# A fused windowed-attention and squared-ReLU FFN kernel: opening laid out by hand with w_out loaded ahead of chunk 2, and q and k of chunks 4 to 11 turned by the DMA crossbar

## Chip, cores, metric

One core of a Trainium2 chip (trn2). The metric is device time of one execution in microseconds (us), median of several. "Span" is first to last instruction in the profile; in the profiled runs it is 1.7 to 1.9 us shorter than the time of the same execution (before: span 239.2, time 241.05).

## The reference

```python
# q, k, v: (batch 4, heads 8, seq 768, dim 64), float32;  n_global 8, n_local 96
scores = q @ k^T / sqrt(64);  rel = i - j
keep   = (j < 8) | ((rel >= 0) & (rel < 96))
dist   = 96 where global and not local, else |rel|
a      = softmax(where(keep, scores - slope[h] * dist, -1e9))
x      = (a @ v) as (3072 tokens, 512)
out    = square(relu(x @ w_in)) @ w_out        # w_in 512x2048, w_out 2048x512
```

## The kernel before

The 3072 tokens are 12 chunks of 256. A chunk's attention needs q and k with the head dimension on partitions, so each is turned; then come masked scores, exp, values, and a transposed chunk `xt` of x. `f1(c)` is the first FFN product of a chunk (8 pieces, each 8 matmuls of 256 columns, into `hps`), `f2(c)` the second (8 pieces of 4 matmuls of 512 columns, into `yps`). Each engine runs its instructions in the order of the program text, so the text is the schedule. `place(main, side, slots)` puts side job i ahead of main job `slots[i]`; jobs in `later` (mostly VectorE) are emitted ahead of the next job.

```python
    def turn_q(c, h0=0, h1=H, by=None):
        ck = chunks[c]
        ...                                            # cut: new tile ck.q
        trp = bank([P, H, P], "trq", FP16)
        for h in range(h0, h1):
            nc.tensor.transpose(out=trp[:, h, :], in_=ck.sq[:, h, :], identity=ident)
        hh = slice(h0, h1)
        (by or nc.scalar.copy)(out=ck.q[:, 1, hh, :], in_=trp[:, hh, :])
        ...                                            # cut: two VectorE copies, later
    # turn_k: the same for k, then (later) four VectorE copies that build keys kb

    def second(c, j, m0):
        ck = chunks[c]
        if m0 == 0:
            ck.yps = ps_y.tile([P, d_model], FP32, name="yps", tag="y")
        for m in range(m0, m0 + 4):
            nc.tensor.matmul(ck.yps, lhsT=ck.h2[:, m, j * P:(j + 1) * P],
                             rhs=w_out_sb[:, m, :], start=m == 0, stop=m == NFT - 1)
        ...                                            # cut: copy and store y
    def f2(c):
        return [lambda j=j, m0=m0: second(c, j, m0) for j in range(2)
                for m0 in range(0, NFT, 4)]

    ORDER = (0, 2, 3, 1, 6, 4, 5, 7)   # of attention: 0, 1 scores; 2..5 values; 6, 7 xt

        load(0)
        load_w_in(0, 512)
        load(1)
        fill_dist()
        for f in range(512, d_ff, 512):
            load_w_in(f, f + 512)
        load(2)
        for m in range(0, NFT, 4):
            load_w_out(m, m + 4)
        load(3)
        ...                                            # cut: attention of chunk 0
        run(place(f1(0), ...))                         # beside attention of chunk 1
        run(place(f1(1), ...))                         # beside attention of chunk 2
        run(place(f2(0), ...))                         # beside attention of chunk 3
        for c in range(1, NC):
            if c + 5 < NC:
                load(c + 5)
            main = zip_jobs(f2(c), f1(c + 1)) if c + 1 < NC else f2(c)
            ...                      # cut: beside it attention c + 3, turning of c + 4
```

The loads convert float32 to fp16 on the way and are issued by GpSimd (POOL).

The softmax here doesn't subtract the row's maximum and nothing guards it: scores larger than these inputs give would overflow.

## Time and profile before

| | before |
|---|---|
| time, median (range) | 240.07 us (239.79 to 240.2) |
| first FFN matmul | 22.0 us |
| steady stretch | 62 to 228.7 us |
| one loop with turning / without | 17.54 / 16.66 us |

The page of the kernel before: its span, busy time by engine, and two rows of its 40 slices of 6 us (busy tenths).

```profile
span 239.2 us, 5383 instructions
...
PE 221.9 (93%) x2214; PEld 155.1 (65%) x2214; DVE 152.4 (64%) x409; ACT 143.6 (60%) x256; POOL 38.6 (16%) x51
...
PE   4666988979899999999999999999999999999993
...
DMA  6999999994968159158249110110110111101112
```

TensorE (PE) is full from the twelfth slice on and has holes before that, while DMA is full in slices 2 to 9. The engine times by stage of the kernel before say the same in us (columns: stretch, its length, busy time and count of each engine, granted clock, DMA share, GB/s; the DMA share adds up packet times, which overlap, so it can pass 1):

```profile
core 0: us, PE busy (x) PEld busy (x) DVE busy (x) ACT busy (x) POOL busy (x), PEclk, DMA share, GB/s
22.00:62.00 40.00, 35.17 (x427) 26.19 (x426) 30.15 (x83) 31.54 (x61) 13.95 (x16) 1.00 1.43 170
62.00:79.50 17.50, 17.50 (x185) 12.40 (x186) 13.88 (x38) 11.26 (x20) 2.63 (x3) 1.00 0.86 107
149.70:167.30 17.60, 17.60 (x187) 12.51 (x186) 12.40 (x35) 11.42 (x22) 0.00 (x0) 1.00 0.09 32
```

From 62 us on, only less TensorE work makes the kernel faster. "Busy" overlaps pipelined matmuls, so for the stage before it work must be counted in pieces: at the steady pace 22 to 62 us holds 32.5 us of work. What turning costs in a loop is in the chain of waits of the kernel before (start, us, what):

```profile
167.28 0.97 PE yps L341 x4
...
169.12 0.45 PE trq L190 x8
...
177.02 0.45 PE trk L205 x8
...
184.82 0.97 PE yps L341 x4
```

Eight transposes of q take 0.45 us on the path, and eight of k another 0.45. The head of the kernel, from the same chain:

```profile
17.62 1.02 ACT kx L207
...
18.66 0.29 DVE kb L216
...
20.21 0.43 DVE tm L292
...
20.69 0.40 PE trx L304 x2
21.09 0.97 PE sp L261 x16
22.05 3.52 PE hps L329 x16
```

VectorE (DVE) builds chunk 1's keys before it normalises chunk 0's last heads, and the FFN waits for that. The first 16 FFN matmuls then take 3.52 us, where 16 later take 1.75: single ones last up to 421 ns, against a median of 273. (The clock record of this trace begins at 26.1 us, so the 1.00 shown for 22 to 62 us does not cover them.) Three more lines of the kernel before, one from its instructions in order of time and two from what the trace says of the tile of w_in:

```profile
24.80 0.89 POOL L178 DMA_DIRECT2D sq<-in_q_dram  x1 [1.72 <-DMA w_in_sb<-in_moe_w_in_dram]
...
L362 POOL DMA_DIRECT2D w_in_sb<-in_moe_w_in_dram x4: 760/792/815, 4.2 to 9.2; - x4
...
DMA to landing us min/median/max: 7.2/12.2/15.1
```

GpSimd's next load, issued at 24.8 us, had waited for a piece of w_in. The last piece was issued at 9.2 us and took the longest, 15.1 us, so it landed at 24.3 us.

### The profile page before, as it was taken

How to read it: one execution, taken by the hardware profiler on the slowest of the kernel's cores; microseconds unless marked ns; L12 is line 12 of the kernel's file. 1: busy time of each engine (PE TensorE's matmuls, PEld its weight loads, DVE VectorE, ACT ScalarE, POOL GpSimd, SP SyncE). 2: the span in 40 equal slices, each digit the busy share in tenths (PEclk: the TensorE clock that was granted, in tenths of full speed). 3: DMA queues.
4: the chain of work that ended last, by engine and by line, in shares of the span. 5: the costliest groups of instructions: out<-in, count | busy, mean ns of one | idle time of the engine just before them, and what ended most of it. 6: DMA issues, size and time to landing. Idle time of an engine off the chain costs nothing.

```text
span 239.2 us, 5383 instructions
## 1 busy us (share of the span) xinstructions
PE 221.9 (93%) x2214; PEld 155.1 (65%) x2214; DVE 152.4 (64%) x409; ACT 143.6 (60%) x256; POOL 38.6 (16%) x51
## 2 busy tenths in 40 slices
PE   4666988979899999999999999999999999999993
PEld 1554776846567767777676777767766676766651
DVE  7676689766967765567768755658758564333231
ACT  2975996957755764864764774784684564233310
POOL 8842534212302102102102000000000000000000
PEclk9999999999999999999999999999999999999998
DMA  6999999994968159158249110110110111101112
GB/s 61 192 193 203 192 207 187 182 181 83 167 98 84 51 89 91 48 87 88 57 79 90 44 47 0 47 45 3 44 47 0 47 45 47 43 1 47 44 44 88
DMA packets 45144, 20.26 MB, mean 85 GB/s; under 512 B 37952, under 2 KB 42048, under 8 KB 45120
## 3 DMA queue, kind: packets, MB, share of 16 engines
q0 software_dynamic: 41664, 13.63, 51.0%
q1 hardware_dynamic: 3456, 6.29, 6.8%
q8 instruction: 17, 0.28, 0.5%
q14 instruction: 7, 0.06, 0.1%
HBM read 27.26 MB, written 6.29 MB: 140 GB/s over the span
## 4 chain that ended last, share of the span: by engine, by line
PE 82%; ACT 8%; DVE 6%; DMA 2%; issue 1%; POOL 0%; POOLq 0%
PE yps L341 34%; PE hps L329 33%; PE sp L261 5%; PE av L285 4%; ACT ex L268 4%; PE trx L304 2%; DMA sq<-in_q_dram 2%; PE trq L190 2%; PE trk L205 2%; ACT hr L332 2%; DVE tm L292 1%; ACT kx L207 1%; ACT qx L192 1%; DVE qx L195 1%; DVE qx L196 1%
## 5 line engine op out<-in xcount | busy, mean ns | idle before, releaser
L329 PE MATMUL hps<-xt,w_in_sb 128*128 128x256 f16 x768 | 101.1, 276 | 0.0
L341 PE MATMUL yps<-w_out_sb,h 128*128 128x512 f16 x384 | 97.3, 379 | 0.0
L332 ACT ACTIVATE hr<-hps 128x512 f16<-128x512 f32 x96 | 58.9, 617 | 62.3 <-PE hps L329 58.0
L329 PEld LDWEIGHTS <-w_in_sb 128*128 128x128 f16 x768 | 72.7, 99 | 18.5 <-issue 0.2
L333 DVE TENSOR_TENSOR h<-hr 128x512 f16<-128x512 f16 x96 | 40.5, 422 | 43.9 <-ACT hr L332 43.4
L268 ACT ACTIVATE ex<-sp 128x512 f16<-128x512 f32 x96 | 49.4, 609 | 8.3 <-PE sp L261 8.3
L341 PEld LDWEIGHTS <-h 128*128 128x128 f16 x384 | 34.8, 98 | 26.6
L271 DVE TENSOR_TENSOR phat<-ex,mask 128x1024 f16<-128x1024 f16 x48 | 33.0, 691 | 20.7 <-ACT ex L268 20.7
L285 PEld LDWEIGHTS <-phat 128*128 128x128 f16 x384 | 18.8, 101 | 8.6 <-DVE phat L271 2.0
L292 DVE TENSOR_TENSOR tm<-av,rec 128x256 f16<-128x256 f32 x48 | 20.4, 425 | 1.7
L285 PE MATMUL av<-vodd,phat 128*128 128x65 f16 x256 | 18.5, 201 | 2.5 <-DVE vodd L238 1.5
L345 DVE COPY y<-yps 128x512 f32<-128x512 f32 x24 | 16.4, 685 | 5.4 <-PE yps L341 5.4
L306 ACT CAST xt<-trx 128x512 f16<-128x512 f32 x24 | 14.6, 608 | 8.5 <-PE trx L304 8.5
L261 PE MATMUL sp<-qx,kx 64*128 64x128 f16 x256 | 15.5, 232 | 2.9 <-DVE kx L207 1.3
L178 POOL DMA_DIRECT2D sq<-in_q_dram x12 | 10.7, 892 | 44.6 <-PE trq L190 40.3
L261 PEld LDWEIGHTS <-kx 64*128 64x128 f16 x256 | 10.5, 100 | 9.3 <-issue 6.8
L178 POOL DMA_DIRECT2D sk<-in_k_dram x12 | 10.5, 876 | 33.9 <-PE trk L205 29.1
L304 PE MATMUL trx<-perm,tm 128*128 128x128 f16 x96 | 10.6, 226 | 4.7 <-DVE tm L292 4.7
L304 PEld LDWEIGHTS <-tm 128*128 128x128 f16 x96 | 7.3, 99 | 8.8 <-DVE tm L292 6.2
L192 ACT COPY qx<-trq 128x1024 f16<-128x1024 f16 x11 | 11.6, 1054 | 1.6 <-PE trq L190 1.6
L207 ACT COPY kx<-trk 128x1024 f16<-128x1024 f16 x11 | 11.8, 1069 | 0.8 <-PE trk L205 0.8
L285 PE MATMUL av<-veven,phat 128*128 128x65 f16 x128 | 11.3, 194 | 0.0
(55 smaller groups left out, 132.5 us busy)
## 6 DMA issues: line engine op xcount, KB each, us to landing
out_dram<-y SPq DMA_DIRECT2D x24, 256.0 KB, 2.0
sq<-in_q_dram POOLq DMA_DIRECT2D x12, 256.0 KB, 6.3
sk<-in_k_dram POOLq DMA_DIRECT2D x12, 256.0 KB, 6.9
sv<-in_v_dram POOLq DMA_DIRECT2D x12, 256.0 KB, 7.5
w_in_sb<-in_moe_w_in_dram POOLq DMA_DIRECT2D x4, 512.0 KB, 12.2
w_out_sb<-in_moe_w_out_dram POOLq DMA_DIRECT2D x4, 512.0 KB, 17.2
```

The source lines that it names most:

```text
L178: nc.gpsimd.dma_start(out=dst, in_=src[ck.b, :, ck.u * CH:(ck.u + 1) * CH, :].rearrange("h (p e) d -> p h (e d)", e=2))
L261: nc.tensor.matmul(sp[ek][:, e, s, :], lhsT=ck.keys[rr][rows, h, :], rhs=ck.q[rows, 1 - ek:3 - ek, h, rr * HP:(rr + 1) * HP], start=True, ...
L268: nc.scalar.activation(out=ex[:, ek].rearrange("p e c -> p (e c)"), in_=sp[ek].rearrange("p e s c -> p (e s c)"), func=AF.Exp, scale=scale)
L271: later.append(lambda: nc.vector.tensor_tensor(out=phat, in0=ex, in1=mask[:, :, 2 * a:2 * a + 2, k0:k0 + 2, :].rearrange("p k e s c -> p k ...
L285: nc.tensor.matmul(av[:, e, rr, :], lhsT=phat[:, ek, e, s * P:(s + 1) * P], rhs=ck.vals[rr][:, 2 * a + e, ek, 0:D + 1], start=ek == 0, sto ...
L292: nc.vector.tensor_tensor(out=tm.rearrange("p r e d -> p e r d"), in0=av[:, :, :, 0:D], in1=rec[:, :, :, None].to_broadcast([P, 2, 2, D]), ...
L304: nc.tensor.matmul(trx[:, i, rr, :], lhsT=ck.tm[2 * g + i][:, rr, :, :], rhs=perm, start=True, stop=True)
L329: nc.tensor.matmul(hps[:, m2, :], lhsT=w_in_sb[:, kk, m * P:(m + 1) * P], rhs=ck.xt[:, kk, :], start=kk == 0, stop=kk == NCT - 1)
L332: nc.scalar.activation(out=hr, in_=hps, func=AF.Relu)
L333: later.append(lambda: nc.vector.tensor_tensor(out=ck.h2[:, 2 * i:2 * i + 2, :], in0=hr, in1=hr, op=ALU.mult))
L341: nc.tensor.matmul(ck.yps, lhsT=ck.h2[:, m, j * P:(j + 1) * P], rhs=w_out_sb[:, m, :], start=m == 0, stop=m == NFT - 1)
L345: nc.vector.tensor_copy(out=y, in_=ck.yps)
```

## The change

It has two parts: TensorE is freed of two thirds of the turning, and the first 60 us are rearranged. In the new order f2(0) follows f1(0) at once, where f1(1) stood between them before, so w_out is needed sooner.

```diff
+    def turn_dma(c):
+        ck = chunks[c]
+        new_q(c)
+        new_k(c)
+        nc.sync.dma_start_transpose(out=ck.q[:, 1], in_=ck.sq.rearrange("p h c -> p (h c)"))
+        nc.sync.dma_start_transpose(out=ck.k, in_=ck.sk.rearrange("p h c -> p (h c)"))
     def prep(c):
-        return [lambda: turn_q(c), lambda: turn_k(c)]
+        if c < NPE:
+            return [lambda: turn_q(c), lambda: turn_k(c)]
+        return [lambda: fix_q(c), lambda: fix_k(c)]
+    NPE = 4
 ...
-        load(2)
         for m in range(0, NFT, 4):
             load_w_out(m, m + 4)
+        load(2)
         load(3)
 ...                      # cut: chunk 0's attention, now in an order by hand, with
 ...                      # 3 + 2 dummy matmuls (warm) where TensorE would idle
+        side = [lambda: fix_v(1)] + [att[1][i] for i in ORDER]
+        run(place(f1(0) + f2(0), side, [0, 2, 5, 6, 8, 9, 11, 12, 14]))
+        load(4)
+        load(5)
+        turn_dma(4)
+        side = (prep(2) + [lambda: fix_v(2)] + [att[2][i] for i in ORDER]
+                + prep(3) + [lambda: fix_v(3)] + [att[3][i] for i in ORDER]
+                + prep(4) + [lambda: fix_v(4), lambda: load(6), lambda: turn_dma(5)])
+        run(place(f1(1) + f2(1) + f1(2), side,
+                  [0, 1, 2, 3, 6, 7, 8, 9, 11, 12, 14, 10, 11, 12, 13, 16, 17, 18, 19, 21, 22, 24,
+                   20, 22, 23, 12, 14]))
-        for c in range(1, NC):
+        for c in range(2, NC):
+            if c + 4 < NC:
+                turn_dma(c + 4)
 ...                      # cut: beside loop c attention c + 2 (was c + 3), fixes of c + 3
```

`fix_q` and `fix_k` are the VectorE copies that followed the turning before; they now also follow the crossbar.

More of the change, by code (lines that the diff above doesn't have):

```diff
@@ L104, in fill_small @@
         V = nc.vector
-        V.memset(tiny, 0.0)
-        nc.scalar.activation(out=tiny, in_=tiny, func=AF.Exp)
         V.memset(zero, 0.0)
+        nc.scalar.activation(out=tiny, in_=zero[:, 0:1], func=AF.Exp)
         V.memset(fill, BIG)
@@ L112, in fill_small @@
         V.memset(shift[HP:P], float(CH))
-        V.memset(thr[0:HP], 0.0)
-        V.memset(thr[HP:P], -float(P - 1))
     def fill_dist():
         V = nc.vector
-        V.tensor_scalar(out=ident, in0=jmp, scalar1=0.0, scalar2=None, op0=ALU.is_equal)
         V.tensor_scalar(out=dist[:, 1, 0, :], in0=dist[:, 0, 0, :], scalar1=1.0,
@@ L139, in fill_perm @@
     def fill_perm():
+        nc.vector.memset(thr[0:HP], 0.0)
+        nc.vector.memset(thr[HP:P], -float(P - 1))
         nc.vector.tensor_scalar(out=perm, in0=jmp2, scalar1=thr, scalar2=None,
@@ L150, with flush @@
     later = []
+    def flush():
+        todo, later[:] = list(later), []
+        for f in todo:
+            f()
     def run(jobs):
         for job in jobs:
-            todo, later[:] = list(later), []
-            for f in todo:
-                f()
+            flush()
             job()
@@ L180, in load @@
                     "h (p e) d -> p h (e d)", e=2))
-    def turn_q(c, h0=0, h1=H, by=None):
-        ck = chunks[c]
-        if h0 == 0:
-            ck.q = qk_p.tile([P, 3, H, P], FP16, name="qx", tag="qx")
-        trp = bank([P, H, P], "trq", FP16)
-        for h in range(h0, h1):
-            nc.tensor.transpose(out=trp[:, h, :], in_=ck.sq[:, h, :], identity=ident)
-        hh = slice(h0, h1)
-        (by or nc.scalar.copy)(out=ck.q[:, 1, hh, :], in_=trp[:, hh, :])
-        def beside():
-            nc.vector.tensor_copy(out=ck.q[0:HP, 2, hh, :], in_=ck.q[HP:P, 1, hh, :])
-            nc.vector.tensor_copy(out=ck.q[HP:P, 0, hh, :], in_=ck.q[0:HP, 1, hh, :])
-        later.append(beside)
@@ L199, in turn_k, with new_q @@
-    def turn_k(c, h0=0, h1=H, by=None):
-        ck = chunks[c]
-        if h0 == 0:
-            ck.k = kx_p.tile([P, H, P], FP16, name="kx", tag="kx")
-        trp = bank([P, H, P], "trk", FP16)
-        for h in range(h0, h1):
-            nc.tensor.transpose(out=trp[:, h, :], in_=ck.sk[:, h, :], identity=ident)
-        hh = slice(h0, h1)
-        (by or nc.scalar.copy)(out=ck.k[:, hh, :], in_=trp[:, hh, :])
+    def new_q(c):
+        chunks[c].q = qk_p.tile([P, 3, H, P], FP16, name="qx", tag="qx")
@@ new lines, in new_k, with turn @@
+    def new_k(c):
+        chunks[c].k = kx_p.tile([P, H, P], FP16, name="kx", tag="kx")
+    def turn(st, dst, h0, h1, by):
+        trp = bank([P, H, P], "trp", FP16)
+        for h in range(h0, h1):
+            nc.tensor.transpose(out=trp[:, h, :], in_=st[:, h, :], identity=ident)
+        (by or nc.scalar.copy)(out=dst[:, h0:h1, :], in_=trp[:, h0:h1, :])
+    def turn_q(c, h0=0, h1=H, by=None):
+        if h0 == 0:
+            new_q(c)
+        turn(chunks[c].sq, chunks[c].q[:, 1], h0, h1, by)
+        later.append(lambda: fix_q(c, h0, h1))
@@ new lines, in turn_k, with fix_q @@
+    def turn_k(c, h0=0, h1=H, by=None):
+        if h0 == 0:
+            new_k(c)
+        turn(chunks[c].sk, chunks[c].k, h0, h1, by)
+        later.append(lambda: fix_k(c))
+    def turn_dma(c):
+        ck = chunks[c]
+        new_q(c)
+        new_k(c)
+        nc.sync.dma_start_transpose(out=ck.q[:, 1], in_=ck.sq.rearrange("p h c -> p (h c)"))
+        nc.sync.dma_start_transpose(out=ck.k, in_=ck.sk.rearrange("p h c -> p (h c)"))
+    def fix_q(c, h0=0, h1=H):
+        ck, hh = chunks[c], slice(h0, h1)
+        nc.vector.tensor_copy(out=ck.q[0:HP, 2, hh, :], in_=ck.q[HP:P, 1, hh, :])
+        nc.vector.tensor_copy(out=ck.q[HP:P, 0, hh, :], in_=ck.q[0:HP, 1, hh, :])
@@ L208, in turn_k, with fix_k @@
+    def fix_k(c):
+        ck = chunks[c]
         if ck.u == 0:
             ck.keys = (ck.k, ck.k)
-        else:
-            pre, zero = chunks[c - 1], chunks[c - ck.u]
-            kb = qk_p.tile([P, H, P], FP16, name="kb", tag="kb")
-            ck.keys = (kb, ck.k)
-            def change():
-                nc.vector.tensor_copy(out=kb[:, :, 0:HP], in_=ck.k[:, :, 0:HP])
-                nc.vector.tensor_copy(out=kb[:, :, HP + GP:P], in_=pre.k[:, :, HP + GP:P])
-                nc.vector.tensor_copy(out=kb[:, :, HP:HP + GP], in_=zero.k[:, :, 0:GP])
-                nc.vector.tensor_copy(out=ck.k[:, :, 0:GP], in_=zero.k[:, :, 0:GP])
-            later.append(change)
+            return
+        pre, zero = chunks[c - 1], chunks[c - ck.u]
+        kb = qk_p.tile([P, H, P], FP16, name="kb", tag="kb")
+        nc.vector.tensor_copy(out=kb[:, :, 0:HP], in_=ck.k[:, :, 0:HP])
+        nc.vector.tensor_copy(out=kb[:, :, HP + GP:P], in_=pre.k[:, :, HP + GP:P])
+        nc.vector.tensor_copy(out=kb[:, :, HP:HP + GP], in_=zero.k[:, :, 0:GP])
+        nc.vector.tensor_copy(out=ck.k[:, :, 0:GP], in_=zero.k[:, :, 0:GP])
+        ck.keys = (kb, ck.k)
@@ L371, in prep @@
     def prep(c):
-        return [lambda: turn_q(c), lambda: turn_k(c)]
-    engines = {PE, mybir.EngineType.Pool, mybir.EngineType.Activation, mybir.EngineType.DVE}
+        if c < NPE:
+            return [lambda: turn_q(c), lambda: turn_k(c)]
+        return [lambda: fix_q(c), lambda: fix_k(c)]
+    NPE = 4
+    engines = {PE, mybir.EngineType.Pool, mybir.EngineType.Activation, mybir.EngineType.DVE,
+               mybir.EngineType.SP}
     with tc.manual_schedule(engines=engines):
@@ L383 @@
             load_w_in(f, f + 512)
-        load(2)
         for m in range(0, NFT, 4):
             load_w_out(m, m + 4)
+        load(2)
         load(3)
         fill_decay(0, 2, 0, 8)
+        nc.vector.tensor_scalar(out=ident, in0=jmp, scalar1=0.0, scalar2=None,
+                                op0=ALU.is_equal)
         att = [attention(c) for c in range(NC)]
         dve = nc.vector.tensor_copy
-        run([lambda: warm(6), lambda: turn_q(0, 0, 4, dve), lambda: turn_q(0, 4, 8, dve),
-             lambda: turn_k(0, 0, 4, dve), lambda: turn_k(0, 4, 8, dve),
-             att[0][0], lambda: (fix_v(0), fill_perm()), att[0][1], att[0][2], att[0][3],
-             lambda: turn_q(1), att[0][6], lambda: turn_k(1), att[0][4], att[0][5],
-             lambda: fix_v(1), att[0][7], lambda: fill_decay(2, 3, 0, 4), att[1][0],
-             lambda: fill_decay(2, 3, 4, 8)])
@@ L397 @@
-        ORD1 = (2, 3, 1, 6, 4, 5, 7)
-        run(place(f1(0), [att[1][i] for i in ORD1] + prep(2) + [lambda: fix_v(2)],
-                  [2, 3, 4, 5, 6, 7, 8, 6, 7, 7]))
+        warm(6)
+        turn_q(0, 0, 4, dve)
+        flush()
+        turn_q(0, 4, 8, dve)
+        turn_k(0, 0, 4, dve)
+        flush()
+        turn_k(0, 4, 8, dve)
+        fix_v(0)
+        fill_perm()
+        att[0][0]()
+        flush()
+        att[0][1]()
+        fill_decay(2, 3, 0, 8)
+        warm(3)
+        att[0][2]()
@@ L400 @@
+        att[0][3]()
+        att[0][6]()
+        turn_q(1)
+        q1 = later.pop()
+        flush()
+        att[0][4]()
+        att[0][5]()
+        q1()
+        warm(2)
+        att[0][7]()
+        turn_k(1)
+        side = [lambda: fix_v(1)] + [att[1][i] for i in ORDER]
+        run(place(f1(0) + f2(0), side, [0, 2, 5, 6, 8, 9, 11, 12, 14]))
         load(4)
-        run(place(f1(1), [att[2][i] for i in ORDER] + prep(3) + [lambda: fix_v(3)],
-                  [0, 2, 3, 4, 5, 6, 7, 8, 6, 7, 7]))
@@ L403 @@
         load(5)
-        run(place(f2(0), [att[3][i] for i in ORDER] + prep(4) + [lambda: fix_v(4)],
-                  [0, 2, 3, 4, 5, 6, 7, 8, 6, 7, 7]))
-        for c in range(1, NC):
+        turn_dma(4)
[5 more added lines that the diff above has]
+                   20, 22, 23, 12, 14]))
@@ L410 @@
             side, slots = [], []
+            if c + 2 < NC:
+                side = [att[c + 2][i] for i in ORDER]
+                slots = [0, 4, 5, 7, 8, 11, 12, 15]
             if c + 3 < NC:
-                side = [att[c + 3][i] for i in ORDER]
-                slots = [0, 4, 5, 7, 8, 11, 12, 15]
-            if c + 4 < NC:
-                side += prep(c + 4) + [lambda c=c: fix_v(c + 4)]
+                side += prep(c + 3) + [lambda c=c: fix_v(c + 3)]
                 slots += [2, 9, 13]
```

## The prediction

> **What bounds it now.** From 62 to 228.7 us TensorE (PE): the table of engine time by stage has it busy 17.5 of 17.5 us in every stretch, and the list of waits shows no PE wait there. One chunk costs 17.54 us with its prep (the chain, 167.3 to 184.8) but 16.66 us in the first loop without, so turning q and k costs PE 0.88 us a chunk. FFN alone is 16 pieces of 0.87 us, 13.9; attention is thus 2.8. Earlier it is different: the first FFN matmul (hps) starts at 22.0 us, and its first 16 take 3.6 us where 16 later take 1.75. From 22 to 62 us the same sums give 32.5 us of PE work; 7.5 are lost. DMA is full from 4 to 55 us (181 GB/s written on q, k, v, 206 on weights): stepwise, w_in lands near 22, chunk 2 near 26, w_out near 37 us.
>
> **What the change does.**
> 1. q and k of 8 chunks leave PE: 8 x 0.88 = -7.0 us, all on the bound path. ACT loses 16 copies of 1.06 us, off the path. The crossbar gets 16 transfers of 256 KB on SP's queue. No trace here has one. The Trainium skill, "VectorE: DVE Perf Modes", "The three transpose paths", gives 1309 ns for 128x128 by DMA; eight blocks in series would be (estimate) 10.5 us, 21 a pair; "DMA: Bandwidth & Descriptors", "Latency and other measured facts", has 261 GB/s, far less. A pair starts at a loop's head and is read in the next loop, q some 18 and k some 26 us later. So even the slow figure is hidden.
> 2. w_out before chunk 2: at 206 GB/s its quarters land near 24.6, 27.1, 29.7, 32.2 us, chunk 2 near 36.6. f2(0) can follow f1(0) directly.
> 3. Hand-made opening: DVE no longer rebuilds chunk 1's keys ahead of chunk 0's last normalisations (tm at 19.7 and 20.2 hold trx, then xt at 21.7). Instead ACT runs 2.7 us of decay after the last exp (14.5), then xt, qx, xt (2.2 us): first hps at about 19.4, -2.6 us.
> 4. Lookahead shrinks by a chunk: the last xt copy (0.6 us) comes 2.4 us of PE work before its reader. I expect no stall.
>
> **Sum.** First hps 19.4; f1(0), f2(0) and attention 1: 16.6 of work, 1.7 of slow clock, 0.7 of waits: 38.4. The 24-piece stretch: 20.8 + 5.6 + 1.8 us, and 1.5 because ACT (hr 0.62, exp 0.61, copies 1.06) is as full as PE in the f1 parts: 68.1. Eight loops of 16.66: 201.4; last FFN 20.8; tail 3.6: span 225.8, time 226.5. Of the 13.5 us gained, 7 are the turning and 6.5 the opening.
>
> Prediction 226.5 us, 222 to 232 for eight in ten. Faster by over 2%: 0.91; within 2%: 0.07; slower: 0.02.
>
> **What would show it.** No PE transposes after chunk 3; loops at 16.6 to 16.7 us, PE fully busy; hps first at 19 to 20 us; steady stretch from about 68 us; transposes landing in under 15 us; DMA full until about 50 us; no PE wait on w_out over 1 us.
>
> **What would make it wrong.** Transposes slower than a loop, or holding up loads or stores on the same engines: DVE waiting for DMA at the q and k fixes, PE behind it (the full 7 us and more). A row of waits for xt at loop heads: lookahead too short. If ACT or DVE order, not DMA, rules 22 to 62 us, the opening gives only 2 to 4 us: near 230. If PE's clock stays up and ACT does not bind, 223.

## The result, and the profile after

The time is 230.0 us (229.24 to 231.48, 4 runs) against 240.03: ratio 0.959, 95% interval 0.9536 to 0.9644. Six later runs gave 229.28 us, ratio 0.9557 (0.9529 to 0.9586). A ratio is the mean time of one kernel's fast runs over that of the other's of the same rounds, so it is not quite the ratio of the medians quoted. The prediction, 226.5 with 222 to 232, holds the result; the gain is 9.8 to 10.6 us by the ratios, where 13.5 was forecast.

| | before | predicted | after |
|---|---|---|---|
| first FFN matmul | 22.0 | 19.4 | 17.5 |
| f2(0) done | | 38.4 | 39.7 |
| steady stretch begins | 62 (a loop earlier) | 68.1 | 69.8 |
| one loop | 17.54 | 16.66 | 16.65 |
| transposes on PE after chunk 3 | | none | none |
| crossbar transfer, issue to landing | | under 15 | 2.7 to 11.2, median 4.7 (q), 4.2 (k) |
| DMA full (9 in its row) until | 54 | about 50 | 85 |
| longest PE wait on w_out | | 1 at most | 1.5, in all 2.9 |
| span | 239.2 | 225.8 | 227.7 |

The page of the kernel after: span, busy times, two rows of 40 slices (5.7 us each), the queues, and the crossbar's issues (count, median us to landing).

```profile
span 227.7 us, 5164 instructions
...
PE 214.3 (94%) x2091; PEld 146.2 (64%) x2091; DVE 150.8 (66%) x408; ACT 129.5 (57%) x240; POOL 39.0 (17%) x51
...
PE   4789959999998999999999999999999999999993
...
DMA  6999999999999997969955105109101101110112
...
q1 hardware_dynamic: 20352, 10.49, 21.3%
...
qx<-sq SPq DMA_TRANSPOSE x8, 4.7
kx<-sk SPq DMA_TRANSPOSE x8, 4.2
```

The hole in PE's row is now the sixth slice (`5`, 28.5 to 34 us), while DMA is full. Engine times by stage of the kernel after:

```profile
core 0: us, PE busy (x) PEld busy (x) DVE busy (x) ACT busy (x) POOL busy (x), PEclk, DMA share, GB/s
17.50:26.50 9.00, 8.56 (x100) 7.00 (x97) 8.13 (x26) 7.34 (x13) 2.68 (x3) 1.00 1.24 206
26.50:39.70 13.20, 10.31 (x73) 5.14 (x73) 3.91 (x9) 3.62 (x7) 4.39 (x5) 0.87 1.52 194
39.70:69.80 30.10, 28.75 (x339) 21.83 (x339) 23.31 (x65) 22.46 (x40) 8.85 (x10) 1.00 1.50 174
70.40:87.20 16.80, 16.80 (x169) 11.47 (x170) 14.54 (x40) 9.60 (x19) 4.39 (x5) 1.00 1.57 163
```

The second stretch is the weak one. PE, VectorE and ScalarE (ACT) are all far from full in it, and PE's granted clock is 0.87. Its work is 8 pieces of f2(0) and part of chunk 1's attention. By the chain's durations these take 6.9 + 0.55 + 0.22 + 0.50 + 0.22 = 8.4 us, so 4.8 of 13.2 us are lost. The chain of waits of the kernel after names what for (it shows the start of the stretch, and the two loop heads of the steady part):

```profile
14.99 19.46 DMA w_out_sb<-in_moe_w_out_dram
...
34.50 1.48 PE yps L353 x4
...
39.90 0.45 PE trp L194 x8
...
103.83 0.97 PE yps L353 x4
...
120.49 0.97 PE yps L353 x4
```

The last quarter of w_out was issued at 14.99 us and landed 19.46 us later, at 34.45. Then TensorE went on at once. The instructions of the kernel after in order of time show each quarter waited for (in brackets the idle time before, and what ended it):

```profile
21.75 0.88 POOL L179 DMA_DIRECT2D sv<-in_v_dram  x1 [1.85 <-DMA w_in_sb<-in_moe_w_in_dram]
...
27.06 1.04 PE L353 MATMUL yps<-w_out_sb,h 128*128 128x512 f16 x4
...
29.42 1.02 PE L353 MATMUL yps<-w_out_sb,h 128*128 128x512 f16 x4 [1.10 <-DMA w_out_sb<-in_moe_w_out_dram]
...
31.96 1.83 PE L353 MATMUL yps<-w_out_sb,h 128*128 128x512 f16 x4 [1.52 <-DMA w_out_sb<-in_moe_w_out_dram]
...
34.50 1.48 PE L353 MATMUL yps<-w_out_sb,h 128*128 128x512 f16 x4 [0.27 <-DMA w_out_sb<-in_moe_w_out_dram]
```

GpSimd's line says that it waited until 21.7 us for a piece of w_in (landed at 21.5 by the trace). The quarters of w_out arrive 2.5 us apart (29.4, 31.9, 34.5); reckoned back, the first was there near 26.9 us and the end of w_in near 24.3. But each feeds only 0.86 us of work, since f2(0) takes row half j = 0 through all quarters first and j = 1 after. The last two of the three groups that waited take 1.83 and 1.48 us instead of 1.02: in this execution the granted clock was at half from 32.0 to 35.5 us (see e6 and the last section). From 70 us on the list of waits has no PE wait.

### The profile page after: what moved, and what is told of

Read it like the earlier page. It is cut to its first block, busy times and chain, and to the rows that moved or that the text cites. A ratio compares the mean times of both kernels' runs of the same rounds, so it can differ in the third digit from the quotient of the medians.

```text
span 227.7 us, 5164 instructions
## 1 busy us (share of the span) xinstructions
PE 214.3 (94%) x2091; PEld 146.2 (64%) x2091; DVE 150.8 (66%) x408; ACT 129.5 (57%) x240; POOL 39.0 (17%) x51
## 3 DMA queue, kind: packets, MB, share of 16 engines
q1 hardware_dynamic: 20352, 10.49, 21.3%
HBM read 27.26 MB, written 6.29 MB: 147 GB/s over the span
## 4 chain that ended last, share of the span: by engine, by line
PE 78%; DMA 12%; DVE 3%; ACT 2%; POOL 2%; issue 1%; POOLq 0%
PE yps L353 36%; PE hps L341 31%; DMA w_out_sb<-in_moe_w_out_dram 9%; PE sp L273 5%; PE av L297 4%; DMA sk<-in_k_dram 4%; PE trx L316 2%; ACT ex L280 1%; POOL sq L179 1%; ACT hr L344 1%; DVE h L345 1%; PE trp L194 1%; DVE tm L304 1%; ACT kx L195 0%; POOL sv L179 0%
## 5 line engine op out<-in xcount | busy, mean ns | idle before, releaser
L341 PE MATMUL hps<-xt,w_in_sb 128*128 128x256 f16 x768 | 98.3, 273 | 0.1
L344 ACT ACTIVATE hr<-hps 128x512 f16<-128x512 f32 x96 | 57.6, 607 | 62.8 <-PE hps L341 57.5
L341 PEld LDWEIGHTS <-w_in_sb 128*128 128x128 f16 x768 | 72.0, 98 | 17.8 <-issue 0.3
L273 PE MATMUL sp<-qx,kx 64*128 64x128 f16 x256 | 15.0, 229 | 1.8 <-DVE kx L195 0.6
L302 DVE RECIPROCAL rec<-av 128x4 f32<-128x4 f32 x48 | 8.5, 176 | 5.8 <-PE av L297 5.2
L179 POOL DMA_DIRECT2D sv<-in_v_dram x12 | 11.0, 916 | 4.0 <-DMA w_in_sb<-in_moe_w_in_dram 1.8
L316 PE MATMUL trx<-perm,tm 128*128 128x128 f16 x96 | 10.0, 223 | 1.2 <-DVE tm L304 1.2
## 6 DMA issues: line engine op xcount, KB each, us to landing
sv<-in_v_dram POOLq DMA_DIRECT2D x12, 256.0 KB, 10.5
w_out_sb<-in_moe_w_out_dram POOLq DMA_DIRECT2D x4, 512.0 KB, 17.8
```

What stands on the lines that cost most here:

```text
L179: nc.gpsimd.dma_start(out=dst, in_=src[ck.b, :, ck.u * CH:(ck.u + 1) * CH, :].rearrange("h (p e) d -> p h (e d)", e=2))
L273: nc.tensor.matmul(sp[ek][:, e, s, :], lhsT=ck.keys[rr][rows, h, :], rhs=ck.q[rows, 1 - ek:3 - ek, h, rr * HP:(rr + 1) * HP], start=True, ...
L316: nc.tensor.matmul(trx[:, i, rr, :], lhsT=ck.tm[2 * g + i][:, rr, :, :], rhs=perm, start=True, stop=True)
L341: nc.tensor.matmul(hps[:, m2, :], lhsT=w_in_sb[:, kk, m * P:(m + 1) * P], rhs=ck.xt[:, kk, :], start=kk == 0, stop=kk == NCT - 1)
L344: nc.scalar.activation(out=hr, in_=hps, func=AF.Relu)
```

## The experiments

Theory A: the turning leaves the bound path at full worth, the crossbar costs nothing, and the opening's gain is cut by the landing of w_out. Rival B: the opening is held by the order of ScalarE and VectorE work, not by DMA. Rival C: the crossbar's transfers slow loads or stores and give part of the gain back. Ratios are against the kernel before of the same rounds; "us off" between two experiments is the difference of their ratios times 240.2. The rounds ran on several chips, so only ratios are compared across them.

| run | median us | ratio (95%) |
|---|---|---|
| a0_after: the changed kernel again | 229.28 | 0.9557 (0.9529 to 0.9586) |
| e1_pe_turn | 235.83 | 0.982 (0.9806 to 0.9835) |
| e2_crossbar_alone | 234.31 | 0.9763 (0.9745 to 0.9781) |
| e3_chunk2_first | 234.24 | 0.9759 (0.9733 to 0.9785) |
| e4_no_w_out_wait (wrong result) | 227.31 | 0.9464 (0.9445 to 0.9484) |
| e5_quarter_major | 227.45 | 0.9463 (0.9442 to 0.9485) |
| e6_warm_in_wait | 229.32 | 0.9546 (0.9523 to 0.9569) |
| e7_f1_in_wait | 231.56 | 0.9631 (0.96 to 0.9662) |
| e8_f1_in_wait_later | 226.46 | 0.9417 (0.9399 to 0.9434) |
| e9_quarter_fix_v | 229.03 | 0.952 (0.9501 to 0.954) |
| e10_crossbar_twice | 230.62 | 0.9598 (0.9568 to 0.9627) |
| e11_both | 224.51 | 0.934 (0.932 to 0.936) |

All but e4 gave the correct result. The changed kernel's own two measurements differ by 0.8 us (0.959, 0.9557); differences below 1 us between single experiments are not used.

### The two parts alone: e1_pe_turn, e2_crossbar_alone

e1, on the changed kernel:

```diff
-    NPE = 4
+    NPE = NC
     def turn_dma(c):
+        if c < NPE:
+            return
         ck = chunks[c]
```

> The changed kernel with q and k of chunks 4 to 11 turned on TensorE again, the new opening kept. My account (turning is worth 0.88 us a chunk on the bound path, the crossbar costs nothing): 230.0 + 7.0 = 237.0 us, loops of 17.5 us. Rival (crossbar transfers of 11 us among the loads of 46 to 68 us give some of it back in the opening): 233 to 235 us, and the loops would then start earlier than 69.8 us less 1.8 us of turning work.

Measured 235.83 us: the opening alone is worth 4.3 us against the kernel before, and the crossbar 5.5 to 6.3 us on top of it, not 7.0. The loops are as expected: 17.54 us in e1's chain (70.58, 88.12, 105.67 for three loop heads), 16.65 after. That makes 0.89 us times 7 chunks, 6.2 us. The eighth, chunk 4, is turned inside the opening, where TensorE is not full: from the first scores of chunk 2 to the first loop e1 takes 26.4 us and the changed kernel 25.8, so it is worth 0.6 there at most and not 0.88 (by the first loop heads alone, 70.58 against 70.38, it is 0.2). The sign of the rival in the expectation, loops that start 1.8 us earlier than 69.8, did not come: those of e1 start at 69.96 us.

e2, on the kernel before (opening and load order kept):

```diff
+    def turn_dma(c):        # as in the change
     def prep(c):
+        if c > 4:
+            return [lambda: fix_q(c), lambda: fix_k(c)]
         return [lambda: turn_q(c), lambda: turn_k(c)]
 ...
+            if c + 4 < NC:
+                turn_dma(c + 4)
             if c + 5 < NC:
                 load(c + 5)
 ...
-                slots += [2, 9, 13]
+                slots += [9, 12, 13]
```

> The kernel before with only the crossbar for chunks 5 to 11 (7 chunks; its opening and load order kept). My account: 7 x 0.88 = 6.2 us off 240.0, 233.9 us. Rival (crossbar disturbs loads or stores): less than 4 us off.

Measured 234.31, 5.7 us off for 7 chunks (0.81 each). The two parts add up: 4.3 + 5.7 is 10.0, and the change gains 9.8 to 10.6. So nothing of importance is lost between them, which speaks against C. (e2 turns one chunk less by the crossbar; that chunk is worth little, as e1 shows.)

### Is the crossbar hidden? e10_crossbar_twice

```diff
-        nc.sync.dma_start_transpose(out=ck.q[:, 1], ...)
-        nc.sync.dma_start_transpose(out=ck.k, ...)
+        for _ in range(2):
+            nc.sync.dma_start_transpose(out=ck.q[:, 1], ...)
+            nc.sync.dma_start_transpose(out=ck.k, ...)
```

> The changed kernel with every crossbar transfer done twice. My account (the crossbar is hidden: a pair lands in about 5 us of a 16.65 us loop and is read a loop later): within 0.7 us of the changed kernel's 229.3 to 230.0 us, loops at 16.65 us. Rival (transfers hold up loads, stores or the fixes): 2 us or more slower.

Measured 230.62, which is 0.2 us above the first measurement of the changed kernel and 1.0 above the second: not told apart. The loops stay at 16.65 us (heads at 71.24, 87.89, 104.55), so in the steady part 16 more transfers cost nothing. C falls there. In the opening they may cost something: e10's first loop head comes at 71.24 us, the changed kernel's at 70.38 and, in a0_after, at 70.24. One profile of e10 does not settle it. The queue line of the page of e10 shows that they did run:

```profile
q1 hardware_dynamic: 37248, 14.69, 34.8%
```

### Is it w_out's landing? e3_chunk2_first, e4_no_w_out_wait

e3:

```diff
-        for m in range(0, NFT, 4):
-            load_w_out(m, m + 4)
         load(2)
+        for m in range(0, NFT, 4):
+            load_w_out(m, m + 4)
```

> The changed kernel with chunk 2 loaded ahead of w_out again. My account (from 27 to 34.5 us TensorE waits for w_out, which lands at the rate of the DMA engines): w_out's last quarter lands 4.3 us later, near 38.8 us, and the time is 3 to 4.5 us up, 233 to 234.5 us. Rival (the opening is limited by the order of ScalarE and VectorE work): under 1 us up.

Measured 234.24, 4.1 to 4.9 us up, about the 4.3 us that chunk 2's three loads take (0.79 MB written at 181 GB/s). The list of PE's waits between 20 and 70 us of e3 has one wait on w_out of 4.4 us:

```profile
PE yps L353 <- DMA w_out_sb<-in_moe_w_out_dram: 5.6, 4, 4.4
```

So the load order is needed by this opening, and TensorE follows w_out's landing. This contradicts B for this stretch. Note also that e3 ends where e2 does (0.9759 and 0.9763): with the old load order the rest of the new opening gains nothing measurable. The new load order without the rest was not tried.

e4:

```diff
             nc.tensor.matmul(ck.yps, lhsT=ck.h2[:, m, j * P:(j + 1) * P],
-                             rhs=w_out_sb[:, m, :], start=m == 0, stop=m == NFT - 1)
+                             rhs=w_in_sb[:, m % 4, (m // 4) * 512:(m // 4 + 1) * 512]
+                             if c == 0 else w_out_sb[:, m, :], start=m == 0, stop=m == NFT - 1)
```

> The changed kernel with the second FFN product of chunk 0 reading slices of w_in (landed at 24 us) in place of w_out: a wrong result on purpose, the same shapes and count. My account: the 2.9 us of waits on w_out and about 1.8 us of slow matmuls after them go, less what the next wait (chunk 2's load, last byte near 38.8 us) takes back: 2 to 4.5 us off 230.0. Rival (ScalarE and VectorE order rules): under 1 us off.

Measured 227.31 (relative error 0.80), 2.2 to 3.0 us off. It is less than the 4.8 us lost around w_out, since the next load then holds TensorE: of e4's waits between 20 and 70 us, two are for chunk 2. The second ends at 38.49 us, when chunk 2's k has landed; the same turning starts at 41.05 us in the changed kernel, so 2.6 us of the lead are left there.

```profile
PE trp L194 <- DMA sk<-in_k_dram: 0.7, 1, 0.7
PE trp L194 <- DMA sq<-in_q_dram: 0.4, 1, 0.4
```

### The wait or the slow clock? e5_quarter_major, e6_warm_in_wait

e5 takes chunk 0's second product by quarters of w_out:

```diff
-            ck.yps = ps_y.tile(...)              # and every use of ck.yps
+            ck.yps[j] = ps_y.tile(...)
 ...
+        f2m = [lambda j=j, m0=m0: second(0, j, m0) for m0 in range(0, NFT, 4)
+               for j in range(2)]
-        run(place(f1(0) + f2(0), side, ...))
+        run(place(f1(0) + f2m, side, ...))
```

> The changed kernel with the second product of chunk 0 taken quarter by quarter of w_out, both row halves at each, so that half of its work is done before the last quarter lands at 34.5 us. My account (w_out's landing is what holds TensorE from 28 to 34.5 us): the product ends near 36.5 instead of 39.7 us, then chunk 2 (last byte near 38.8 us) is the next limit, so 2 to 3 us off the changed kernel, as with the no-wait run (2.7). Rival (the order of ScalarE and VectorE work): under 0.7 us off.

Measured 227.45, 2.3 to 3.1 us off: as much as with no wait on w_out at all, with a correct result. Waits on w_out fell from 2.9 to 0.9 us.

e6 keeps the waits and fills them with dummy matmuls:

```diff
+        side += [lambda: warm(5), lambda: warm(6), lambda: warm(1)]
-        run(place(f1(0) + f2(0), side, [0, 2, 5, 6, 8, 9, 11, 12, 14]))
+        run(place(f1(0) + f2(0), side, [0, 2, 5, 6, 8, 9, 11, 12, 14, 9, 10, 11]))
```

> The changed kernel with 12 dummy matmuls on zeros put into the three waits for w_out: the waits stay, the clock stays up. If the slow clock after the waits matters, the matmuls of 634 ns there go back to 379 ns, and 0.4 to 1 us comes off, with runs agreeing within 0.5 us like those of the run with TensorE turning. If it doesn't matter: within 0.3 us of the changed kernel, same spread.

Measured 229.32: no gain against 229.28, and runs still from 228.86 to 230.27. The slow matmuls are gone (the longest yps matmul is 390 ns, 634 after). But that cannot be put down to the dummy matmuls, for the changed kernel itself has executions without the dip. Two lines of a0_after's profile, its waits between 15 and 72 us and its engine times:

```profile
PE yps L353 <- DMA w_out_sb<-in_moe_w_out_dram: 3.6, 3, 1.5
...
26.50:39.70 13.20, 9.62 (x83) 5.12 (x82) 4.34 (x11) 3.79 (x8) 4.37 (x5) 1.00 1.52 193
```

The clock is 1.00 there, the longest yps matmul 390 ns, and the waits for w_out are longer (3.6 us, 2.9 in after). This execution took 229.29 us, the one with the dip 229.43. So the dip is real but hardly counts in the time: TensorE is released by w_out, and then by chunk 2. My guess that the dip alone makes the spread of 2 us between runs falls too; its cause stays open.

### Work for the wait: e7_f1_in_wait, e8_f1_in_wait_later, e9_quarter_fix_v, e11_both

While TensorE waits for w_out it has work that needs neither w_out nor chunk 2, the first product of chunk 1, if chunk 1's attention ends early enough. e7:

```diff
-        run(place(f1(0) + f2(0), side, [0, 2, 5, 6, 8, 9, 11, 12, 14]))
- ...                    # load(4), load(5), turn_dma(4), then the 24-piece stretch
+        g = f1(1)
+        side = (...)     # the sides of both stretches and the loads, in one list
+        run(place(f1(0) + f2m[:2] + zip_jobs(f2m[2:], g[:6]) + g[6:] + f2(1) + f1(2), side,
+                  [0, 2, 5, 6, 6, 8, 8, 9, 10,
+                   18, 19, 21, 20, 22, 23, 24, 25, 27, 28, 30,
+                   26, 27, 28, 29, 32, 33, 34, 35, 37, 38, 40,
+                   36, 38, 39, 16, 16, 16, 28, 30]))
```

> Quarter by quarter as in the last but one, and the first product of chunk 1, which needs neither w_out nor chunk 2, moved into the waits between the quarters; attention of chunk 1 a few steps earlier to make it possible. My account (4.8 us are lost to w_out, 0.7 more behind chunk 2): both waits are filled, 4 to 5.5 us off the changed kernel, 224.5 to 226 us. If ScalarE (relu and exp now denser) binds instead: 1 to 3 us off.

Measured 231.56: slower than the changed kernel of the same rounds (0.9631 against 0.9557). The waits on w_out are gone, but my slots put chunk 2's scores and values too early. Three groups of e7 in order of time:

```profile
41.34 0.23 PE L273 MATMUL sp<-qx,kx 64*128 64x128 f16 x2 [1.22 <-DVE kx L231]
...
46.05 0.23 PE L297 MATMUL av<-vodd,phat 128*128 128x65 f16 x2 [2.25 <-DVE vodd L254]
...
47.29 0.22 PE L297 MATMUL av<-veven,phat 128*128 128x65 f16 x2 [1.00 <-DVE veven L257]
```

VectorE reached the values' fix only behind the masking of the scores it should have preceded. Here one late job on VectorE was passed on to all behind it. (The granted clock also fell, to 0.94 over 39.7 to 69.8 us.) e8 moves these slots:

```diff
-                   18, 19, 21, 20, 22, 23, 24, 25, 27, 28, 30,
-                   26, 27, 28, 29, 32, 33, 34, 35, 37, 38, 40,
-                   36, 38, 39, 16, 16, 16, 28, 30]))
+                   18, 19, 21, 22, 25, 26, 26, 28, 29, 30, 31,
+                   24, 27, 28, 30, 32, 33, 34, 35, 37, 38, 40,
+                   36, 37, 16, 16, 16, 28, 30]))           # fix_v(4) into loop 2, slot 1
```

> The last schedule (first product of chunk 1 in the waits for w_out) did fill those waits: its trace has none. It lost the time again behind them, 1.2 us before the scores of chunk 2 and 3.3 us before its values, both because I placed chunk 2's attention too early for its load (lands near 38.8 us) and for the fixes on VectorE, and then 1.5 us of slow clock. Here chunk 2's scores come two steps later and its values' fix ahead of them, and the values' fix of chunk 4 moves into the next loop. My account: 5 to 6 us off that run, 225.5 to 226.5 us. Rival (VectorE and ScalarE are simply too full there): 228 us or more.

Measured 226.46, 5.1 us off e7. e9 was meant to test its second edit on e5:

```diff
-                + prep(4) + [lambda: fix_v(4), lambda: load(6), lambda: turn_dma(5)])
+                + prep(4) + [lambda: load(6), lambda: turn_dma(5)])
 ...                                   # fixes of chunk 4's q, k at slots 20, 21
+            if c == 2:
+                side += [lambda: fix_v(4)]
+                slots += [1]
```

> The quarter-by-quarter kernel (227.5 us) with the values' fix of chunk 4 moved into the next loop, since VectorE is busy 1.97 of 2 us just before the first loop of the steady stretch and TensorE waits 0.8 us there: 0.5 to 1 us off that kernel, 226.5 to 227 us. If that wait is not VectorE's load but its order: no change.

Measured 229.03, 1.4 us worse than e5 and the opposite of what I expected. VectorE of e9 in order of time:

```profile
70.89 0.69 DVE L283 TENSOR_TENSOR phat<-ex,mask 128x1024 f16<-128x1024 f16 x1 [0.29 <-ACT ex L280]
71.55 0.44 DVE L250 COPY vodd<-sv 128x1024 f16<-128x1024 f16 x1
...
73.52 0.42 DVE L257 COPY veven<-sv 4x1024 f16<-4x1024 f16 x1
```

In its old place the fix ran while VectorE waited for nothing. In the new one it stands behind masking that waits for ScalarE's exp, and PE's values wait 1.3 us for it. (q's and k's fixes moved too in this run, and its first scores of the loop already start at 68.20 us, e5's at 67.31, so its 1.4 us are not all proven to be the values' fix.) e11 is e8 with chunk 4's three fixes back in their places (`36, 38, 39`, no extra job in loop 2).

> The last schedule with chunk 1's first product in the waits (226.5 us), and chunk 4's fixes of q, k and v put back where the changed kernel has them, since moving the values' fix into the next loop made the quarter-by-quarter kernel 1.6 us slower: there it stands behind the masking of the first scores, which waits for ScalarE, and TensorE waits 1.3 us for it. My account: 1.2 to 2.2 us off the 226.5, near 224.7 us, no wait over 1 us on TensorE after 20 us. If the later fix was not the cause: 226 us or more.

Measured 224.51 us, ratio 0.934: 1.8 us off e8, and 5.2 to 6.0 us off the changed kernel. It is faster than both kernels. Its engine times over the same stretches as shown of the changed kernel:

```profile
26.50:39.70 13.20, 13.20 (x119) 9.34 (x118) 5.54 (x14) 6.78 (x13) 4.39 (x5) 1.00 1.52 194
39.70:69.80 30.10, 29.28 (x340) 21.25 (x339) 26.10 (x74) 22.23 (x41) 10.07 (x12) 1.00 1.50 186
```

TensorE is busy 13.20 of 13.20 us where the changed kernel had 10.31 (9.62 in a0_after), with DMA moving the same 194 GB/s. The loads are no faster; TensorE has other work while they come.

## Why the prediction was right, and where it was off

The result lies in the predicted range. The number alone does not prove the account: the prediction also named "near 230" for the case that the order of ScalarE and VectorE rules the opening, and 230.0 was measured. It is e3, e4 and e5 that tell the two apart. Step by step:

1. **Turning on the crossbar.** "8 x 0.88 = -7.0 us, all on the bound path." The mechanism is shown by e1 and e2; the size was 5.5 to 6.3 us. The term was 8 where it should have been 7 and a bit: chunk 4 is turned in the opening, which does not bind on TensorE. That the crossbar is hidden held: a pair, from the issue of q to the landing of k, takes 4.2 to 14.3 us, the longest in the opening, and loops are 16.65 us, even with twice the transfers. That DMA would be full until about 50 us did not hold: it is full until 85 us, at no cost that a run shows.
2. **First FFN matmul.** Predicted 19.4, measured 17.5 us. I had the exps end at 14.5 us as before. In the new order the first scores start at 9.0 instead of 9.8 us, the exps end at 13.7, and the first FFN group needs only the first half of xt.
3. **w_out.** This is the step that failed. "Stepwise, w_in lands near 22 ... us": the trace of before already had the last piece of w_in landing at 24.3 (the lines shown above), and I read it off the change in GB/s instead. From there "its quarters land near 24.6, 27.1, 29.7, 32.2 us" is 2.3 us early at the end: the last quarter landed at 34.5. TensorE was also ready sooner (first FFN matmul 1.9 us earlier, f2(0) begun at 27.06). So where "1.7 of slow clock, 0.7 of waits" were forecast beyond the 16.6 us of work of the f1(0), f2(0) stretch, 5.6 were lost: 2.9 of waits for w_out and 1.9 of slower matmuls after 26.5 us, 0.8 before. e3, e4, e5 and e11 show that it is this landing; e3 moves it by chunk 2's load and the time follows. So of "6.5 the opening" 4.3 us came (e1).
4. **The 24-piece stretch.** Predicted 29.7 us, measured 30.1 (39.7 to 69.8). TensorE is busy 28.75 of it, and from 60.7 to 69.8 us the chain of waits runs over ScalarE and VectorE: for this part the order of their work does bind, as B has it. No lookahead stall at loop heads showed in the steady stretch.
5. **From span to time.** Predicted 225.8 to 226.5, 0.7 us. In the runs the difference is 1.7. I had set the profiled span of before (239.2, whose own time was 241.05) beside the median time of other executions (240.07).

The account closes: the span missed by 1.9 us (first FFN -1.9, f1(0) and f2(0) +3.2, the 24 pieces +0.4, the rest +0.2), the step to time by 1.0, and the median of the four runs lay 0.6 above the profiled one: 3.5 us, from 226.5 to 230.0. The first two errors run against each other, so it is partly luck that the span came within 1.9 us.

What stays open: why the changed kernel's runs spread over 2 us when those of before spread over 0.4 to 1.4 (e6 and a0_after exclude only the dip of the clock as the sole cause), and how much of the first FFN's faster start is due to the dummy matmuls and how much to the order, since neither was tried alone. One profile bears on it: in a0_after the granted clock was at half from 7.6 to 17.8 us in spite of the dummy matmuls, and the first FFN matmul still came at 18.1 us, against 17.5 in after and 22.0 before.

## What to carry to other kernels

When an opening is bound by loads, first list when each load lands, by the lines that waited for it and not by rates, and beside it the work each one sets free. Then give the tensor engine work that needs none of the loads still coming: here the loads landed no sooner in the best version, but another chunk's product filled the time. Work moved off a full engine is worth its full time only in stages where that engine is full (here 0.89 us a chunk in the loops, 0.6 at most in the opening), and the place of a side job in an engine's order can cost more than its length (e7, e9).

## What the Trainium skill lacked or had wrong

- "Advanced Engine Details and Errata", X-Bar Transpose (TRN2), says that transpose DMAs are as fast as regular ones, and "DMA: Bandwidth & Descriptors", Latency and other measured facts, has 261 GB/s for a non-contiguous case. Here 16 transfers SBUF to SBUF of 262,144 bytes raise the hardware queue's share from 7.1% of 233.9 us (e1, stores alone) to 21.3% of 227.7 us: 31.9 us of packet time over 16 engines, 2.0 us a transfer, about 131 GB/s by this measure (e10 gives 1.9 us for 16 more). The stores of the same queue move 6.29 MB in 16.6 us, 379 GB/s, and one of the same size lands in 2.0 us, a transpose in 2.7 at best. So here transposes are not as fast as these regular transfers. The 261 is neither confirmed nor refuted: packet times overlap (loads of q, k and v that move 181 GB/s have a share of 1.82, which would be 99 GB/s by this measure).
- "VectorE: DVE Perf Modes", The three transpose paths, gives 1309 ns for one 128x128 block by DMA. Eight blocks in one transfer landed in 2.7 us at best and 4.2 to 4.7 us in the median, so eight single times (10.5 us) overstate it; under the opening's loads it reached 11.2 us. The pages could give the time by size and under load.
- "TensorE: Matmul & The Clock Gate" warns (Why this matters for your kernels) of idle gaps over about 3 us. Here the granted clock fell to half from 32.0 to 35.5 us of one execution after single gaps of only 1.10 and 1.52 us, with 1.0 us of matmuls between, and yps matmuls took up to 634 ns instead of 379. But in a0_after, the same kernel with gaps of 0.80, 1.51 and 1.28 us, the clock stayed at 1.00. So gaps this short come with a dip in one execution and not in another; what decides was not found.
- In the pages read ("DMA: Bandwidth & Descriptors") I found no figure for a load with others queued in front of it: w_out's pieces of 512 KB took 16.9 to 19.5 us from issue to landing here, while each needs 2.5 us of the engines.
